# A strided sum over eight places in place of three sums over halves, in a sliding attention beside a feed-forward block

## The chip, the cores and the metric

The kernel runs on one core of a Trainium2 chip. The metric is the time of one execution on the device in microseconds (us), as the median of several runs. Engines are named as in the profile: PE is TensorE (matmuls; PEld are its weight loads, which overlap them), DVE is VectorE, ACT is ScalarE, POOL is GpSimd and SP is SyncE, which issues DMAs.

## What is computed

A block with two parallel branches on normalised rows, both in fp32 (2048 rows of 576, 32 heads of 18, a hidden width of 4608):

```python
xn = layernorm(x)
out = x + A(xn) + B(xn)

# A: each row attends to itself and the 7 rows 2, 4, ... 14 before it
idx = pos[:, None] - 2 * arange(8)[None, :]
logits = einsum("bhsd,bhswd->bhsw", q, k[:, :, idx]) * 18 ** -0.5   # -1e9 where idx < 0
attn = softmax(logits, axis=-1)
o = einsum("bhsw,bhswd->bhsd", attn, v[:, :, idx])
A = o_in_rows @ wo

# B
h = relu(xn @ w1 + b1) ** 2
B = h @ w2 + b2
```

The change concerns the line with `o`: for each row and each of its 576 columns, eight products of a weight and a value are summed.

## The kernel before

**Matmuls.** The rows are four blocks `b` of 512. All matrix products run on PE in a 32-bit form in which an operand is split into a high part (a rounded copy, made by ACT) and a low part (the rest, made by a subtraction on DVE); a product is the sum of high by high, high by low and low by high. The split of each weight tile therefore puts one ACT and one DVE instruction ahead of PE. The feed-forward part takes two blocks at a time and builds their first product from seven sub-products of halves instead of eight (`ffn_pair`, with `product` at L629 and `left` at L635); the second product is in `add` (L536). A pair of row blocks and a pair of hidden tiles make one call of `ffn_pair`, 18 calls for each half of the rows. The matmuls of L536 for one row block run beside these calls, seven at a time (`work(0)` to `work(3)`), and those of the other row block follow in loops of their own (`phase_b0` and `phase_b1`), 14 matmuls to a hidden tile.

**Handovers from DVE to PE** that the prediction speaks of:
- In `ffn_pair`, three PSUM banks `ba`, `bb` and `bc` hold the sub-products. DVE reads `bc` twice, at L725 (`r1`, the third sub-product added) and at L752 (`r0`). PE writes `bc` again at the B22 product (L745), right behind the first of these reads, and at the T1 product (L664) of the next call, behind the second. In the profile the reads are `r<-p,r`.
- `w1_lo` (L480) writes the low part of a `w1` tile, `w1s<-w1r,w1s`.
- `w2_lo` (L517) writes the low part of a `w2` or `wo` tile, `w2s<-w2r,w2s`. There are three such buffers. A hidden tile's 14 matmuls read first four high parts and then the low ones, so the fifth is the first that needs DVE's half.

**Attention** runs on DVE between these. The four groups of eight heads (`g`, 144 columns each) of a row block come from DRAM as tiles with four rows j of q to a partition and, for k and v, those and the fourteen rows before them (`fetch`, on POOL's queue). `attention(b, g)` is a generator. For each of four values of j it multiplies q with eight shifted rows of k into `pr` (128 partitions, 8 x 144 elements; `pr<-q,kv`) and reduces over the 18 columns of a head (L387). The softmax follows (L390 to L399). Then, again for each j, it multiplies the weights with eight shifted rows of v into `pr` (`pr<-lg,kv`, L405) and sums the eight places (L408 to L410), which leaves 144 columns in `q`. There is one buffer `pr`. After the fourth j POOL stores the result to DRAM (L415), from where a later step fetches it regrouped.

**Order of the work.** The order on each engine is written out by hand. The generator yields after each product and each sum, and the calls of `side(k)` in the loops (two, three or five between the handovers of a call of `ffn_pair`, one or two for each hidden tile of the loops) take that many units of whichever head group is in turn. The three sums over halves are one unit, as is the multiplication before them. DVE works off its instructions in this order, so a unit that takes longer delays all that stands behind it on DVE.

The helper `tt` (L108) records all two-operand instructions of DVE, so these carry its line and are told apart by their tiles.

Of the kernel before, what the change touches and what calls it, by code (L numbers as in the profile page):

```python
# [12 lines left out]
ALU = mybir.AluOpType  # L13
ET = mybir.EngineType
AX = mybir.AxisListType
# [30 lines left out]
def block_kernel(ctx: ExitStack, tc: tile.TileContext, x, xt, wqkv, wo, w1, b1, w2, b2, w1l, out):  # L46
    nc = tc.nc
# [12 lines left out]
    def kv_tile(n):  # L60
# [25 lines left out]
                            axis=AX.XY, op=ALU.add)  # L86
# [20 lines left out]
    def tt(out, a, b, op):  # L107
        return nc.vector.tensor_tensor(out=out, in0=a, in1=b, op=op)  # L108
# [232 lines left out]
    def shifted(t, j, *dims):  # L341
        a = t[:, j:j + 1, 0:1]
        return bass.AP(tensor=a.tensor, offset=a.offset, ap=[a.ap[0], [DIL * CG, W], *dims])
# [19 lines left out]
    def release():  # L363
        free[0] += 1
        fetch()

    def offer(b, g=None):
        if g is None:
            loads.append(("x", b, None))
            queue.append((("x", b), lambda: statistics(b)))  # L370
        else:
            loads.extend([("k", b, g), ("v", b, g)])
            queue.append((("k", b, g), lambda: attention(b, g)))
        fetch()

    def attention(b, g):
        k, q = landed.pop(("k", b, g)), landed.pop(("q", b, g))
        lg = sb.tile([P, NA, W], F32, name="lg")
        mx = sb.tile([P, NA], F32, name="mx")
        sm = sb.tile([P, NA], F32, name="sm")  # L380
        for j in range(NJ):
            pr = sb.tile([P, W, CG], F32, name="pr")
            tt(pr, q[:, j:j + 1].to_broadcast([P, W, CG]), shifted(k, j, [1, CG]), ALU.mult)
            if j == NJ - 1:
                release()
            yield
            nc.vector.tensor_reduce(out=lg[:, j * HG:(j + 1) * HG].rearrange("p a w -> p w a"),  # L387
                                    in_=pr.rearrange("p w (a d) -> p w a d", d=DH), axis=AX.X, op=ALU.add)
            yield
        if b == 0:  # L390
            l4 = lg[:4].rearrange("p (j h) w -> p j h w", j=NJ)
            tt(l4, l4, mask[:4, :, None].to_broadcast([4, NJ, HG, W]), ALU.add)
        nc.vector.tensor_reduce(out=mx, in_=lg, axis=AX.X, op=ALU.max)
        tt(lg, lg, mx[:, :, None].to_broadcast([P, NA, W]), ALU.subtract)
        yield "exp"
        nc.scalar.activation(lg, lg, AF.Exp, scale=SCALE)
        nc.vector.tensor_reduce(out=sm, in_=lg, axis=AX.X, op=ALU.add)
        nc.vector.reciprocal(sm, sm)
        tt(lg, lg, sm[:, :, None].to_broadcast([P, NA, W]), ALU.mult)  # L399
        yield  # L400
        v = landed.pop(("v", b, g))
        for j in range(NJ):
            pr = sb.tile([P, W, CG], F32, name="pr")
            at = lg[:, j * HG:(j + 1) * HG].rearrange("p a w -> p w a")
            tt(pr.rearrange("p w (a d) -> p w a d", d=DH), at[:, :, :, None].to_broadcast([P, W, HG, DH]),  # L405
               shifted(v, j, [DH, HG], [1, DH]), ALU.mult)
            yield
            tt(pr[:, :4], pr[:, :4], pr[:, 4:], ALU.add)  # L408
            tt(pr[:, :2], pr[:, :2], pr[:, 2:4], ALU.add)
            tt(q[:, j], pr[:, 0], pr[:, 1], ALU.add)  # L410
            if j == NJ - 1:
                for k, (a, z) in enumerate(OPART):
                    rows = oscr[b, k][g * L:(g + 1) * L].rearrange("l (j i) c -> l i j c", i=G)
                    for i in range(G):
                        nc.gpsimd.dma_start(rows[:, i], q[i * L:(i + 1) * L, :, a:z])  # L415
                release()
            yield
# [1203 lines left out]
```

## Time and profile before

| | |
|---|---|
| median of 3 runs | 1107.31 us (1107.31 to 1108.32) |
| profiled execution, its own time | 1107.93 us |
| its span, first to last instruction | 1106.2 us |
| PE busy | 1096.8 us, 99% |
| DVE busy | 912.0 us, 82% |
| ACT busy | 575.0 us, 52% |
| POOL busy | 115.4 us, 10% |
| granted TensorE clock | 1.000 |

A row of a group names line, engine and operation, then `out<-in` by the program's tile names, partitions x elements and type of output and input, and the count; behind the bars stand the busy time in us, the mean of one in ns, and the idle time of the engine just before them with what ended most of it. In a timeline a row begins with the start and the duration in us, rows of equal form are merged (x2 is two instructions), and idle time of over 0.1 us or so ahead of the row is given in brackets with what ended it. A row of the waits reads: who waited, for whom, us in total, times, the longest. A row of a window gives its length, then for PE, PEld, DVE, ACT and POOL the busy us and the number of instructions, then the granted clock, the DMA engines' share and GB/s. In the chain of waits a piece has its start, its length and the number of instructions.

### The profile page before, as it was taken

To read this page: it belongs to the slowest core of one execution; us is meant where nothing else is said; L and a number is where in the kernel's file an instruction comes from. 1 tells how busy PE (TensorE), PEld (TensorE's weight loads), DVE (VectorE), ACT (ScalarE), POOL (GpSimd) and SP (SyncE) were. 2 spreads that over 40 slices of the span, in tenths; PEclk is the share of its full clock that TensorE was granted. 3 is DMA by queue.
4 is the path that set the end of the run, shared out by engine and by line. 5 is a ranking of instruction groups with operands and counts; after the bars stand their busy time and mean duration, and the time that the engine had idled before them with its cause. 6 is when DMAs were issued, how large, how long until landed. Compare 5 with 4: busy or idle time off the path is not lost.

```text
span 1106.2 us, 13892 instructions
## 1 busy us (share of the span) xinstructions
PE 1096.8 (99%) x4950; PEld 925.2 (84%) x4950; DVE 912.0 (82%) x1223; ACT 575.0 (52%) x809; POOL 115.4 (10%) x219
## 2 busy tenths in 40 slices
PE   9999999999999999999999999999999999999998
PEld 7998888888888888888899887888888888888887
DVE  7696979897996979999979488978988789899654
ACT  5435666556566654455344355555555555533342
POOL 4000101020020100100010200202102021000100
PEclk9999999999999999999999999999999999999999
DMA  8956987889699686866755887768686785866752
GB/s 297 329 177 234 333 309 255 296 214 372 229 244 392 220 357 214 311 247 226 259 164 169 309 263 300 259 260 308 238 315 240 267 314 205 316 208 205 280 193 81
DMA packets 100279, 287.83 MB, mean 260 GB/s; under 512 B 13288, under 2 KB 41712, under 8 KB 85488
## 3 DMA queue, kind: packets, MB, share of 16 engines
q1 hardware_dynamic: 65280, 188.15, 49.1%
q0 software_dynamic: 10544, 52.14, 12.9%
q10 hardware_dynamic: 24384, 46.64, 12.6%
q8 instruction: 39, 0.64, 0.2%
q14 instruction: 32, 0.26, 0.1%
HBM read 205.14 MB, written 81.74 MB: 259 GB/s over the span
## 4 chain that ended last, share of the span: by engine, by line
PE 89%; DVE 5%; DMA 3%; ACT 1%; issue 1%; ACTq 0%; POOL 0%; DVEq 0%; POOLq 0%; SPq 0%
PE p L536 46%; PE p L629 31%; PE p L1041 5%; PE p L635 3%; DMA kvq<-st 2%; PE p L338 1%; PE p L1401 1%; PE p L1045 1%; DVE pr L108 1%; DMA kv<-kvq 1%; DVE lg L387 1%; DVE w1r L108 1%; DVE r L108 0%; PE p L1318 0%; DVE h L108 0%
## 5 line engine op out<-in xcount | busy, mean ns | idle before, releaser
L536 PE MATMUL p<-h,w2s 128*128 128x512 f32 x2066 | 491.4, 389 | 0.1
L536 PEld LDWEIGHTS p<-h,w2s 128*128 128x128 f32 x2066 | 387.5, 188 | 81.5 <-ACT h L642 0.6
L629 PE MATMUL p<-X,w1s 128*128 128x512 f32 x864 | 219.7, 389 | 1.2 <-DVE r L108 0.9
L629 PEld LDWEIGHTS p<-X,w1s 128*128 128x128 f32 x864 | 162.0, 188 | 35.6 <-DVE r L108 1.3
L509 ACT ACTIVATE w2s<-w2r 128x640 fp32r<-128x640 f32 x164 | 120.2, 735 | 116.1 <-PE p L536 87.6
L629 PE MATMUL p<-S,w1s 128*128 128x512 f32 x648 | 164.8, 390 | 1.5 <-ACT r L691 1.5
L108 DVE TENSOR_TENSOR w2s<-w2r,w2s 128x576 fp32r<-128x576 f32 x164 | 123.4, 753 | 40.6 <-ACT w2s L509 39.8
L629 PEld LDWEIGHTS p<-S,w1s 128*128 128x128 f32 x648 | 121.4, 188 | 27.4 <-ACT r L691 2.3
L415 POOL DMA_DIRECT2D o<-q x128 | 69.2, 605 | 584.8 <-DVE q L108 582.8
L638 ACT ACTIVATE r<-r,b1t 128x512 f32<-128x512 f32 x72 | 52.0, 723 | 126.9 <-DVE r L108 125.2
L387 DVE TENSOR_REDUCE lg<-pr 128x64 f32<-128x1152 f32 x64 | 86.5, 1352 | 1.5
L108 DVE TENSOR_TENSOR pr<-lg,kv 128x1152 f32<-128x1152 f32 x64 | 86.7, 1354 | 1.3
L108 DVE TENSOR_TENSOR pr<-q,kv 128x1152 f32<-128x1152 f32 x64 | 86.6, 1353 | 0.8
L108 DVE TENSOR_TENSOR pr<-pr 128x576 f32<-128x576 f32 (+1 forms) x128 | 77.5, 605 | 3.2
L646 ACT ACTIVATE r<-r 128x1024 f32<-128x1024 f32 x72 | 76.1, 1057 | 1.2
L108 DVE TENSOR_TENSOR h<-r,h 128x1024 fp32r<-128x1024 f32 (+3 forms) x46 | 51.8, 1136 | 27.0 <-ACT r L646 18.8
L108 DVE TENSOR_TENSOR r<-p,r 128x512 f32<-128x512 f32 (+1 forms) x77 | 52.9, 688 | 20.3 <-PE p L629 9.8
L108 DVE TENSOR_TENSOR w1s<-w1r,w1s 128x1024 fp32r<-128x1024 f32 (+1 forms) x42 | 50.3, 1198 | 16.5 <-ACT w1s L477 16.4
L691 ACT ACTIVATE r<-p 128x512 f32<-128x512 f32 x36 | 21.5, 597 | 70.9 <-PE p L629 70.5
L638 ACT ACTIVATE r<-p,b1t 128x512 f32<-128x512 f32 x72 | 48.3, 672 | 0.0
L108 DVE TENSOR_TENSOR h<-h 128x1024 fp32r<-128x1024 f32 x36 | 43.9, 1220 | 4.8 <-ACT h L938 4.6
L536 PE MATMUL p<-w1s,w2s 128*128 128x512 f32 x195 | 44.7, 389 | 0.0
(193 smaller groups left out, 1174.2 us busy)
## 6 DMA issues: line engine op xcount, KB each, us to landing
w2r<-in_w SPq DMA_DIRECT2D x144, 320.0 KB, 3.4
kv<-kvq POOLq DMA_DIRECT2D x29, 1296.0 KB, 9.4
w<-w1s SPq DMA_DIRECT2D x36, 1024.0 KB, 8.4
w1s<-w ACTq DMA_DIRECT2D x34, 1024.0 KB, 7.3
h<-r SPq DMA_DIRECT2D x36, 512.0 KB, 6.3
h<-h SPq DMA_DIRECT2D x36, 512.0 KB, 4.2
w1r<-in_w SPq DMA_DIRECT2D x18, 640.0 KB, 7.7
kvq<-st ACTq DMA_DIRECT2D x48, 216.0 KB, 3.2
```

The lines of the kernel that those rows point to most:

```text
L108: return nc.vector.tensor_tensor(out=out, in0=a, in1=b, op=op)
L338: nc.tensor.matmul(p[:, :QW], l, r, start=k == 0, stop=k == len(mm) - 1)
L387: nc.vector.tensor_reduce(out=lg[:, j * HG:(j + 1) * HG].rearrange("p a w -> p w a"), in_=pr.rearrange("p w (a d) -> p w a d", d=DH), axis ...
L415: nc.gpsimd.dma_start(rows[:, i], q[i * L:(i + 1) * L, :, a:z])
L509: nc.scalar.activation(w2s[stream[i]][:, :DE], raw2[i], AF.Copy)
L536: nc.tensor.matmul(yp[b][c], v, a, start=c not in yb[b], stop=c in last and c not in [o[0] for o in ops[i + 1:]], skip_group_check=True)
L629: nc.tensor.matmul(to, l, r, start=start and i == 0, stop=i == len(mm) - 1, skip_group_check=True)
L635: nc.tensor.matmul(to, weight(LEFT, k, f), v, start=False, stop=k == 1, skip_group_check=True)
L638: nc.scalar.activation(to, a, AF.Relu, bias=b1t[:, f:f + 1])
L646: nc.scalar.activation(r, r, AF.Square)
L691: nc.scalar.activation(u[:, 0], bb, AF.Copy)
L1041: nc.tensor.matmul(to, l[:, js], r, start=start and n == 0, stop=n == len(mm) - 1, skip_group_check=True)
```

## The change

In the second half of `attention`, the three sums over halves become one reduce:

```diff
             yield
-            tt(pr[:, :4], pr[:, :4], pr[:, 4:], ALU.add)
-            tt(pr[:, :2], pr[:, :2], pr[:, 2:4], ALU.add)
-            tt(q[:, j], pr[:, 0], pr[:, 1], ALU.add)
+            nc.vector.tensor_reduce(out=q[:, j], in_=pr.rearrange("p w c -> p c w"), axis=AX.X, op=ALU.add)
             if j == NJ - 1:
```

Before, the first sum adds places 4 to 7 to places 0 to 3 (576 elements), the second places 2 and 3 to 0 and 1 (288), and the third the last two (144), the first two in place. After, one instruction reads the 1152 elements of `pr` once, for each column its eight places one after the other, and writes 144 sums. Each column's places lie 144 elements, that is 576 bytes, apart. `pr` is no longer overwritten. The order of the eight additions is another one. What runs on PE, ACT, POOL and SP, and in which order, is the same in both kernels; all lines behind L410 move up by two.

On DVE ahead of the first call of `ffn_pair`'s split weights (`w1s` is the split tile of `w1`, `w1r` its source, `pr` the products, `lg` the softmax weights, `kv` the tile of v), before:

```order
L108 TENSOR_TENSOR pr<-lg,kv 128x1152
L108 TENSOR_TENSOR w1r<-w1r 128x512
L108 TENSOR_TENSOR w1r<-w1r 128x256 x2
L108 TENSOR_TENSOR pr<-pr 128x576
L108 TENSOR_TENSOR pr<-pr 128x288
L108 TENSOR_TENSOR q<-pr 128x144
L108 TENSOR_TENSOR w1s<-w1r,w1s 128x1024 x2
```

and after:

```order
L408 TENSOR_REDUCE q<-pr 128x144
L108 TENSOR_TENSOR pr<-lg,kv 128x1152
L108 TENSOR_TENSOR w1r<-w1r 128x512
L108 TENSOR_TENSOR w1r<-w1r 128x256 x2
L408 TENSOR_REDUCE q<-pr 128x144
L108 TENSOR_TENSOR w1s<-w1r,w1s 128x1024 x2
```

The three adds ahead of `w1s` are one reduce in their place, as are the three of the unit before (the first row after).

On DVE within a later call of `ffn_pair`, ahead of a read of bank `bc` (`r_3260<-p_3186,r_3228`, and `r_3222<-p_3152,r_3190` after; the numbers of the buffers differ, since fewer instructions come before), before:

```order
L108 TENSOR_TENSOR pr<-lg,kv 128x1152
L108 TENSOR_TENSOR pr<-pr 128x576
L108 TENSOR_TENSOR pr<-pr 128x288
L108 TENSOR_TENSOR q<-pr 128x144
L108 TENSOR_TENSOR w2s<-w2r,w2s 128x576
L108 TENSOR_TENSOR w1s<-w1r,w1s 128x1024
L108 TENSOR_TENSOR w2s<-w2r,w2s 128x576
L108 TENSOR_TENSOR r_3260<-p_3186,r_3228 128x512
```

and after:

```order
L108 TENSOR_TENSOR pr<-lg,kv 128x1152
L408 TENSOR_REDUCE q<-pr 128x144
L108 TENSOR_TENSOR w2s<-w2r,w2s 128x576
L108 TENSOR_TENSOR w1s<-w1r,w1s 128x1024
L108 TENSOR_TENSOR w2s<-w2r,w2s 128x576
L108 TENSOR_TENSOR r_3222<-p_3152,r_3190 128x512
```

The read of the bank stands behind the same units as before; only the sum itself is another instruction. In the last quarter (`phase_b1`), where units of attention alternate with `w2_lo` and `h_lo` (`h<-h`), the same: three rows become one, and the rest keeps its place.

## The prediction

> **What bounds the kernel now.** I read the page's totals first, then the list of waits for PE alone, then the costs of the operations that the change touches, then timelines at the places where DVE hands something to PE.
>
> The first lines of the page, with busy time and its share of the span for each engine:
>
> ```profile
> span 1106.2 us, 13892 instructions
> PE 1096.8 (99%) x4950; PEld 925.2 (84%) x4950; DVE 912.0 (82%) x1223; ACT 575.0 (52%) x809; POOL 115.4 (10%) x219
> ```
>
> PE is the bound. DVE has 1106 - 912 = 194 us without work, so its own sum could grow a good deal before DVE became the bound as a whole. The change touches DVE alone, so it can shorten the kernel only by shortening what PE waits for. The waits of PE, longest first in total:
>
> ```profile
> PE p L1318 <- DVE lg L1311: 2.1, 1, 2.1
> PE p L629 <- ACT r L691: 1.5, 2, 0.8
> PE p L629 <- DVE r L108: 0.9, 1, 0.9
> PE p L629 <- DVE w1s L108: 0.3, 1, 0.3
> ```
>
> The first stands ahead of all attention. Only the last, 0.3 us, has the changed sums right ahead of it (below). So there is next to nothing to gain on PE, and much to lose: a slower DVE meets a PE that never rests. **The question is what one reduce costs against three adds, and how much of a difference PE's handovers let through.**
>
> **The price of one edit.** 64 times (4 row blocks, 4 head groups, 4 values of j), three adds become one reduce. The rows that bear on it, from the groups with shapes kept apart (count, busy us, mean ns):
>
> ```profile
> L387 DVE TENSOR_REDUCE lg<-pr 128x64 f32<-128x1152 f32 x64 | 86.5, 1352 | 1.5
> L108 DVE TENSOR_TENSOR pr<-pr 128x576 f32<-128x576 f32 x64 | 48.2, 753 | 1.0
> L108 DVE TENSOR_TENSOR pr<-pr 128x288 f32<-128x288 f32 x64 | 29.3, 458 | 2.2
> L108 DVE TENSOR_TENSOR q<-pr 128x144 f32<-128x144 f32 x64 | 19.7, 308 | 2.5 <-DVE pr L108 0.3
> L393 DVE TENSOR_REDUCE mx<-lg 128x32 f32<-128x256 f32 x16 | 6.7, 417 | 0.3
> L1335 POOL TENSOR_TENSOR h<-w1r,h 128x432 fp32r<-128x432 f32 x2 | 2.2, 1118 | 0.0
> ```
>
> Removed: 753 + 458 + 308 = 1519 ns of busy time; with the small gaps between dependent instructions the three hold DVE about 1.6 us (in the rows below the next instruction starts 1.62 us and 1.51 us after the first add). Added: one reduce over 1152 elements. The two reduces of before give its form: (1352 - 417) / (1152 - 256) = 1.04 ns for an element, and 417 - 256 x 1.04 = 150 ns fixed. But both read neighbours: their innermost dimension goes on by 4 bytes. The new one reads `p c w`: its innermost step is from one of the eight places to the next, 144 elements or 576 bytes away, for every element. No row of before reads so.
>
> So the price is bounded. From below: 1.35 us, the same instruction on as many elements with neighbours. No reduce here does better than one element a step of 1.04 ns, so I exclude less. From above: POOL's subtraction streams the slowest, 1118 / 432 = 2.59 ns an element, which would be 2.98 us for 1152. If an element costs whole steps, only two prices lie in between: one step, 1.35 us, and two, 150 + 2 x 1152 x 1.04 = 2.55 us. **I take two steps, 2.55 us**: by its reading pattern the new instruction resembles none of the one-step rows, and 2.55 is the whole-step price nearest to the upper end. This is a choice and not a reading, so one step stays a rival with a large chance. With two steps a sum costs 2.55 - 1.6 = 0.95 us more, 64 x 0.95 = 61 us of DVE in all; with one step 1.35 - 1.6 = -0.25 us, 16 us less.
>
> [...]
>
> **What of 61 us reaches PE.** The instruction order on PE, ACT, POOL and SP is the same before and after; on DVE each three rows become one in place, nothing is moved past a queue, and no wait is added, on PE or elsewhere. POOL's stores of q at L415 wait for the last sum of a head group and start by its lag later; the list of PE's waits above has none on POOL or on a load of attention, so I cost that at nothing; without that cover a head group's first product would come later by the lag. So the loss is DVE's lag behind PE at each handover, less the idle time ahead of it, less the slack with which DVE delivers now.
>
> *First FFN pair.* DVE, then PE (start, duration):
>
> ```profile
> 86.00 1.24 DVE L108 TENSOR_TENSOR pr<-pr 128x576 f32<-128x576 f32 x2
> ...
> 90.41 1.24 DVE L108 TENSOR_TENSOR pr<-pr 128x576 f32<-128x576 f32 x2
> ...
> 91.92 2.40 DVE L108 TENSOR_TENSOR w1s<-w1r,w1s 128x1024 fp32r<-128x1024 f32 x2
> ```
>
> ```profile
> 93.19 1.21 PE L629 MATMUL p<-X,w1s 128*128 128x512 f32 x4 [0.29 <-DVE w1s L108]
> ```
>
> PE waits already, with two sums ahead on DVE and no idle between. Both count in full: 2 x 0.95 = **1.9 us**.
>
> *FFN pairs with three sums ahead of a handover.* A pair's second sum in PSUM bank `bc` is read by DVE (r<-p, L725), and PE may write the bank again only then, at the B22 product (L745). One such pair:
>
> ```profile
> 355.85 1.24 DVE L108 TENSOR_TENSOR pr<-pr 128x576 f32<-128x576 f32 x2
> ...
> 361.58 1.25 DVE L108 TENSOR_TENSOR pr<-pr 128x576 f32<-128x576 f32 x2
> 362.86 0.31 DVE L108 TENSOR_TENSOR q<-pr 128x144 f32<-128x144 f32 x1
> 363.20 1.36 DVE L108 TENSOR_TENSOR pr<-lg,kv 128x1152 f32<-128x1152 f32 x1
> 364.60 1.25 DVE L108 TENSOR_TENSOR pr<-pr 128x576 f32<-128x576 f32 x2
> 365.88 0.31 DVE L108 TENSOR_TENSOR q<-pr 128x144 f32<-128x144 f32 x1
> 366.11 0.75 DVE L108 TENSOR_TENSOR w2s<-w2r,w2s 128x576 fp32r<-128x576 f32 x1
> ...
> 368.58 0.68 DVE L108 TENSOR_TENSOR r<-p,r 128x512 f32<-128x512 f32 x1
> ```
>
> ```profile
> 370.48 1.52 PE L629 MATMUL p<-X,w1s 128*128 128x512 f32 x6
> ```
>
> The read ends at 369.26, PE's next product in the bank starts at 370.48: a slack of 1.2 us. Three sums bring 2.85 us. About 0.4 us of idle time lies between them, so some 2.4 us of lag arrive and about 1.2 us stall PE. There are five such pairs (the reads at 227.13, 297.85, 368.58, 700.58 and 839.81): 5 x 1.2 = **6 us**. Pairs with two sums ahead, or with lag carried over, lose less, for instance
>
> ```profile
> 738.00 1.25 DVE L108 TENSOR_TENSOR pr<-pr 128x576 f32<-128x576 f32 x2
> ...
> 752.55 0.69 DVE L108 TENSOR_TENSOR r<-p,r 128x512 f32<-128x512 f32 x1 [0.30 <-ACT r L723]
> ```
>
> ```profile
> 754.89 1.30 PE L629 MATMUL p<-X,w1s 128*128 128x512 f32 x5
> ```
>
> Three sums (738.00, 741.49, 746.68) less 0.3 us of idle time less 754.89 - 753.24 = 1.65 us of slack: 0.9 us. I count four like it (with the reads at 120.76, 191.26 and 892.17), 1 us each: **4 us**. The other pairs have one sum or none ahead and as much slack, and give nothing.
>
> *The last quarter.* The densest stretch of DVE, then the chain's long piece on PE, then DVE at the first sum and from the last one on:
>
> ```profile
> 978.00:1032.00 54.00, 54.00 (x240) 44.71 (x239) 53.07 (x70) 21.45 (x27) 4.35 (x8) 1.00 0.58 188
> ```
>
> ```profile
> 950.21 150.36 PE p L536 x663
> ```
>
> ```profile
> 978.22 1.24 DVE L108 TENSOR_TENSOR pr<-pr 128x576 f32<-128x576 f32 x2
> ...
> 1030.48 1.24 DVE L108 TENSOR_TENSOR pr<-pr 128x576 f32<-128x576 f32 x2
> 1031.76 0.31 DVE L108 TENSOR_TENSOR q<-pr 128x144 f32<-128x144 f32 x1
> 1031.98 1.42 DVE L108 TENSOR_TENSOR w2s<-w2r,w2s 128x576 fp32r<-128x576 f32 x2
> ```
>
> DVE is busy 53.07 of 54 us (third figure after the length) and PE all 54. Eight sums lie in it: 8 x 0.95 = 7.6 us with nothing to absorb them but slack. PE's 663 matmuls take 150.36 / 663 = 0.227 us each. The first 100 end the third row block (7 + 28 + 65), so tile n of the last one starts at 972.9 + 14 n x 0.227; tile 19 at 1033.2, and its fifth matmul, the first to read the lower half that DVE writes, at 1034.1. DVE finishes that half, the first of the two at 1031.98, at 1032.7. So 1.3 us are left, and 7.6 - 1.3 = **6.3 us** go to PE.
>
> *Between these stages* stand twelve sums (408 to 612 us). Most lie where DVE rests; I count **1 us** there, with 0 and 3 as ends.
>
> Sum: 1.9 + 6 + 4 + 6.3 + 1 = 19.2 us. The profiled execution took 1107.93 us (span 1106.2 and 1.7 around it), 0.6 above the median of 1107.31. 1107.9 + 19.2 = **1127 us**. With all pair terms gone 1107.9 + 9 = 1117; with slack used up by other lags, 2.85 for a three-sum pair and 1.9 for a two-sum one, 1.9 + 14 + 7.6 + 6.3 + 1, that is 31 us, or 1138.
>
> **The rivals.** *One step an element* (ends on the other side: not slower). The reduce then costs what L387 costs, 1352 ns on as many elements. DVE gets 16 us shorter, PE only the 0.29 us at 93.19: 1107.6. It decides from one point: below 1.6 us for the reduce the kernel isn't slower at all. For it speaks that every streaming DVE row above fits 1.04 ns an element; against it, that every one reads neighbours. [...]
>
> *Two steps, but hidden.* DVE's 194 idle us swallow the lag at most handovers, and only the places without idle time pay part: 1109 to 1117, about 1112. Against it: the two places without any idle time, 93.19 and 978 to 1032, give 8 us by themselves.
>
> *More than two steps.* At 2.98 us or above a sum costs 1.4 us more or worse, and since the slack is spent once, most of the extra 0.45 us x 40 sums in dense places goes through: 1127 + 18 = 1145.
>
> That the change does nothing is excluded: the DVE order shows 64 reduces in place of 192 adds.
>
> **How the numbers follow.** Two steps as worked out 0.55 (1117 to 1138); one step 0.31 (1106 to 1109, nearly all within 0.2%, or 2.2 us, which is about what a measurement of this kernel can tell from no change); two steps hidden 0.07; more than two 0.07. The cases of no change and of slower hold most of it, so the range spans both: 1106 to 1138, which leaves out the dearest case. The likeliest one's own range is 1117 to 1138. Faster by over 0.2%: 0.04, part of the one-step case. Within 0.2%: 0.26. Slower by over 0.2%: 0.70.
>
> **What would show it.** The group of the new reduce q<-pr decides first: a mean near 2550 ns is my case, near 1350 ns the rival. Then DVE's busy time (912 + 64 x (2.55 - 1.52) = 978, or 901), new waits of PE on DVE r near the pairs named and on w2s between 978 and 1032, and 1.9 us more at the first pair. If the mean is right and PE's waits sum to far less than 19 us, the slack was misread; if waits stand elsewhere, in ACT's chain behind `r` say, I left out a handover.

## The result, and the profile after

The changed kernel takes **1122.07 us** (median of 4 runs, 1121.79 to 1124.52) against 1107.49 us (1107.31 to 1108.32) for the kernel before on the same chip: a ratio of 1.0134, interval 1.0119 to 1.0149. It is slower by some 14.6 us. The profiled execution took 1121.79 us, with a span of 1120.1.

The page's first lines for the changed kernel, as shown for the one before:

```profile
span 1120.1 us, 13760 instructions
PE 1102.6 (98%) x4950; PEld 925.1 (83%) x4950; DVE 949.6 (85%) x1095; ACT 576.1 (51%) x809; POOL 116.2 (10%) x219
```

DVE grew from 912.0 to 949.6 us, that is 0.59 us for each of the 64 sums. PE's own busy time grew too, from 1096.8 to 1102.6, with the same 4950 matmuls; a part of that is explained below. The group of the new instruction:

```profile
L408 DVE TENSOR_REDUCE q<-pr 128x144 f32<-128x1152 f32 x64 | 139.4, 2178 | 1.0
```

Its mean of 2178 ns is neither one step an element (1352) nor two (2550). And the longest waits of PE, in the form in which they were shown for the kernel before:

```profile
PE p L633 <- DMA w1s<-w: 3.6, 1, 3.6
PE p L534 <- DVE w2s L108: 2.8, 5, 0.9
PE p L627 <- DVE r L108: 2.5, 5, 0.9
PE p L1316 <- DVE lg L1309: 2.1, 1, 2.1
PE p L627 <- ACT r L689: 0.7, 1, 0.7
```

The second and third rows are the lag of DVE that the prediction spoke of (0.9 us of the third was there before). The first is new and no step of the prediction has it: PE waits once, 3.6 us, for a **DMA**.

Since PE works off the same matmuls in the same order in both kernels, the start of each matmul can be compared with its own start before. The difference grows only where time is lost; the last column is its growth since the place above:

| place (time before, us) | difference there, us | grown by |
|---|---|---|
| first FFN pair, 93.19 | +0.1 | 0.09 |
| handover of bank `bc`, 229.04 | +0.5 | 0.43 |
| 273.92, between two of them | +0.9 | 0.42 |
| handovers of bank `bc`, 299.76 and 370.48 | +1.6, +2.1 | 0.61 + 0.56 |
| `add` between the stages, 413 to 544 | +4.2 | 2.06 |
| 630.21, where PE used to wait 0.85 us for ACT | +3.3 | -0.88 |
| **631.70 to 633.64** | **+8.5** | **5.18** |
| handover of bank `bc`, 702.53 | +9.5 | 0.99 |
| last quarter, 996 to 1049 | +13.7 | 4.27 |

**The new wait.** PE's timeline of the changed kernel there:

```profile
633.50 1.52 PE L627 MATMUL p<-S,w1s 128*128 128x512 f32 x6
638.58 1.19 PE L633 MATMUL p<-x,w1s 128*128 128x512 f32 x2 [3.56 <-DMA w1s<-w]
639.57 2.69 PE L627 MATMUL p<-X,w1s 128*128 128x512 f32 x6
...
642.56 1.54 PE L627 MATMUL p<-X,w1s 128*128 128x512 f32 x6
```

Six matmuls of one form take 1.52 us ahead of the wait, 2.69 right behind it, and 1.54 three us later: behind the pause PE runs for a while at about half its rate, which costs another 1.6 us (the difference grows from +6.9 at the wait's end to +8.5). That is where some of PE's additional busy time comes from. The granted clock says the same: 1.00 from 632 to 636 us, and then (third figure from the end)

```profile
636.00:640.00 4.00, 1.42 (x3) 1.14 (x4) 1.88 (x2) 0.00 (x0) 0.00 (x0) 0.83 1.03 398
```

A mean of 0.83 over these four microseconds fits half the clock for 1.4 of them, and PE starts again 1.4 us before their end.

What PE waits for is the second half of a `w1` tile, which `w1_again` (L485, L487 before) loads back on SP's queue in the middle of the program. POOL loads there too: a tile of k (`kv<-kvq`, L360) and the regrouped result of attention (`kv<-o`, L843, L845 before). POOL's timeline before, then SP's issue of the reload with its size and its time to landing:

```profile
616.93 0.77 POOL L360 DMA_DIRECT2D kv<-kvq  x1
617.48 0.76 POOL L845 DMA_DIRECT2D kv<-o  x1
```

```profile
620.49 0.46 SPq L487 DMA_DIRECT2D w1s<-w  x1
```

```profile
w1s<-w SPq DMA_DIRECT2D x1, 1024.0 KB, 11.1
```

It landed at 620.49 + 11.1 = 631.6, and PE used it at once, before:

```profile
631.70 0.70 PE L635 MATMUL p<-x,w1s 128*128 128x512 f32 x2
```

The same two timelines after, and the reload as a piece of the chain (start, length):

```profile
619.40 4.33 POOL L413 DMA_DIRECT2D o<-q  x8 [30.00 <-DVE q L408]
623.52 0.76 POOL L360 DMA_DIRECT2D kv<-kvq  x1
624.16 0.66 POOL L843 DMA_DIRECT2D kv<-o  x1
```

```profile
624.79 0.43 SPq L485 DMA_DIRECT2D w1s<-w  x1
```

```profile
624.79 13.75 DMA w1s<-w
```

POOL's loads stand on its queue behind the eight stores of a head group's result (L413), and these wait for DVE's last sum of that group: the bracket names it. Before, the first load is issued 3.56 us ahead of the reload; after, 1.27 us ahead, since four longer sums lie in the group. POOL's two loads land at 623.9 and 626.4 before, the later of them 5.9 us into the reload, and at 630.3 and 632.7 after, 7.9 us into it. The DMA engines' share is 0.98 to 1.04 from 628 to 640 us (0.99 to 1.05 before, from 620 to 632). The reload takes 13.7 us in place of 11.1, that is 2.6 more. It is also issued 4.3 us later than before, while PE is 3.3 us later there. Since it had no slack, 2.6 + 4.3 - 3.3 = 3.6 us are PE's wait.

### The profile page after: what moved, and what is told of

Its sections match the earlier page's. It is cut to its first block, busy times and chain, and to the rows that moved or that the text cites. A ratio compares the mean times of both kernels' runs of the same rounds, so it can differ in the third digit from the quotient of the medians.

```text
span 1120.1 us, 13760 instructions
## 1 busy us (share of the span) xinstructions
PE 1102.6 (98%) x4950; PEld 925.1 (83%) x4950; DVE 949.6 (85%) x1095; ACT 576.1 (51%) x809; POOL 116.2 (10%) x219
## 4 chain that ended last, share of the span: by engine, by line
PE 68%; DVE 18%; DMA 5%; issue 5%; ACT 3%; DVEq 0%; ACTq 0%; SPq 0%; POOL 0%; POOLq 0%
PE p L534 31%; PE p L627 25%; PE p L1039 6%; DVE pr L108 3%; DVE q L408 3%; DVE h L108 2%; DVE w2s L108 2%; PE p L633 2%; DMA w<-w1s 2%; PE p L338 1%; DVE w1s L108 1%; DVE r L108 1%; DMA w1s<-w 1%; DVE w1r L108 1%; DMA h<-h 1%
## 5 line engine op out<-in xcount | busy, mean ns | idle before, releaser
L408 DVE TENSOR_REDUCE q<-pr 128x144 f32<-128x1152 f32 x64 | 139.4, 2178 | 1.0
L413 POOL DMA_DIRECT2D o<-q x128 | 69.2, 605 | 609.2 <-DVE q L408 607.2
L387 DVE TENSOR_REDUCE lg<-pr 128x64 f32<-128x1152 f32 x64 | 86.5, 1352 | 1.5
```

The lines of the kernel that those rows point to most:

```text
L408: nc.vector.tensor_reduce(out=q[:, j], in_=pr.rearrange("p w c -> p c w"), axis=AX.X, op=ALU.add)
```

## The experiments

My theory A: the sums' own lag accounts for some 10 of the 14.6 us, and the rest is this **collision**, which one head group triggers (the one of row block 1, group 0), whose last sum releases POOL's stores and loads at 612 to 624. The rivals are in the expectations.

**Strided reduce in that head group alone** (four of the 64 sums):

```diff
-            tt(pr[:, :4], pr[:, :4], pr[:, 4:], ALU.add)
...
+            if (b, g) == (1, 0):
+                nc.vector.tensor_reduce(out=q[:, j], in_=pr.rearrange("p w c -> p c w"), axis=AX.X, op=ALU.add)
+            else:
+                tt(pr[:, :4], pr[:, :4], pr[:, 4:], ALU.add)
...
```

> The kernel before, with the strided reduce in the one head group (row block 1, group 0) whose four sums stand right before the regroup loads of the middle stage; all other head groups keep the three adds. Theory A (collision): four sums 0.57 us longer each make POOL's stores and the loads behind them 2.3 us later against PE, these meet the w1 reload on SP's queue, and PE waits 3 us or more for it and then runs some matmuls at half rate: 1110.5 to 1113 us. Rival B (the wait in the middle stage comes from something earlier, or from chance in the DMA queues): within 0.5 us of the kernel before, 1107 to 1108, with no wait of PE on a DMA.

Measured: 1113.97 us against 1108.49 us, ratio 1.0045 (1.0028 to 1.0062). The longest of PE's waits, and the reload as a piece of the chain:

```profile
PE p L638 <- DMA w1s<-w: 4.3, 1, 4.3
```

```profile
622.12 14.47 DMA w1s<-w
```

Four sums that are 0.6 us longer each cost 5.5 us, 1 us above theory A's range and far above B's. A holds: the loss is not spread over the sums. Not all of it is the collision. In the profiled execution (1115.19 us) PE falls back by 2.3 us between 489 and 548 us, which is the four sums' own lag; it gets 1.1 us back at 630, where it used to wait for ACT, and loses 6.8 us at the reload, by the wait and the slow matmuls behind it.

**Strided reduce in all the others** (the same edit with `!=`):

> The changed kernel, with the three adds back in that one head group (row block 1, group 0). Theory A: PE's wait for the w1 reload of 3.6 us and the slow matmuls after it go: 1117 to 1118.5 us. Rival B: as the changed kernel, 1121.5 to 1122.5 us, with the wait still there.

Measured: 1118.04 us against 1108.49, ratio 1.0086 (1.0071 to 1.0101). PE's waits that changed:

```profile
PE p L632 <- DVE r L108: 2.6, 5, 0.9
...
PE p L632 <- ACT r L694: 2.1, 3, 0.8
PE p L539 <- DVE w2s L108: 1.9, 4, 0.6
PE p L632 <- DVE w1s L108: 0.7, 1, 0.7
```

No wait of PE for a DMA is left, and the time lies in theory A's range. The two parts add up, 5.5 + 9.5 = 15.0 us beside 14.6 for the whole change.

**The three adds, and an idle fourth of 432 neighbours** makes the sum as long as the reduce without a strided read:

```diff
             tt(pr[:, :4], pr[:, :4], pr[:, 4:], ALU.add)
+            tt(pr[:, 4:7], pr[:, 4:7], pr[:, 4:7], ALU.add)
             tt(pr[:, :2], pr[:, :2], pr[:, 2:4], ALU.add)
```

> The kernel before, with one more add of neighbours (3 x 144 elements, result not used further) between the first and the second of the three adds of every sum, so that a sum holds DVE about 0.6 us longer, as the strided reduce does, without any strided read. Theory A (only the length of the sum counts): 1120 to 1124 us, with PE's waits at the same places as in the changed kernel. Rival C (the strided read also slows other engines or DMAs at SBUF): under 1115 us.

Measured: 1122.53 us against 1108.49, ratio 1.0126 (1.0111 to 1.0142). The added instruction, and PE's longest wait:

```profile
L108 DVE TENSOR_TENSOR pr<-pr 128x432 f32<-128x432 f32 x64 | 38.9, 608 | 2.2
```

```profile
PE p L636 <- DMA w1s<-w: 4.9, 1, 4.9
```

C falls: the time is that of the changed kernel without any strided read. PE loses time at nearly all the places of the changed kernel, and 1.2 us each at the first FFN pair and at 330.36 (time of before), where the changed kernel loses next to nothing; some handovers lose less. Single places differ by up to 2 us, so a small harm of the strided read beside its length isn't excluded.

**What a strided read costs**, by itself: behind the end of the kernel before, a list of reduces over 8 x 144 elements with the eight places at different distances (lines 1592 to 1610), with other counts of places at 576 bytes (1616, 1617), and products and copies; for instance

```diff
+    [f(out=a, in_=b, axis=X, op=add) for a, b in red(1, 3)]
```

> The kernel before, and behind its end a list of single DVE instructions on unused tiles: reduces of 144 columns over 8 places with the places 1 to 288 elements apart, reduces over 4, 2 and 16 places 144 apart, and products, adds and copies of 1152 elements that read or write far apart. [...] Rival M (banks: the distance of 144 is an unlucky multiple): distances such as 143, 145, 146 or 148 cost nearer 1350 ns than 2180 ns. The products that write 32 bytes apart are open; if writes are free they take 1355 ns.

Measured (the whole took 1360.88 us, which says nothing of the sums). Distances of 4, 8, 12, 16, 576 and 608 bytes, then two and sixteen places, 576 bytes apart:

```profile
L1592 DVE TENSOR_REDUCE q<-kv 128x144 f32<-128x1152 f32 x4 | 5.1, 1346 | 0.0
L1593 DVE TENSOR_REDUCE q<-kv 128x144 f32<-128x1152 f32 x4 | 5.1, 1348 | 0.0
L1594 DVE TENSOR_REDUCE q<-kv 128x144 f32<-128x1152 f32 x4 | 6.7, 1746 | 0.0
L1595 DVE TENSOR_REDUCE q<-kv 128x144 f32<-128x1152 f32 x4 | 8.3, 2148 | 0.0
L1606 DVE TENSOR_REDUCE q<-kv 128x144 f32<-128x1152 f32 x4 | 8.1, 2076 | 0.0
L1610 DVE TENSOR_REDUCE q<-kv 128x144 f32<-128x1152 f32 x4 | 11.4, 2914 | 0.0
L1616 DVE TENSOR_REDUCE q<-kv 128x144 f32<-128x288 f32 x4 | 1.5, 444 | 0.0
L1617 DVE TENSOR_REDUCE q<-kv 128x144 f32<-128x2304 f32 x4 | 15.7, 3994 | 0.0
```

M falls: at distances of 143, 145, 146 and 148 elements the reduce took 2074 to 2078 ns. The dearer price starts with the distance, between 8 and 16 bytes, and is then nearly the same (2074 to 2207 ns) at every distance tried up to 1152 bytes but one (608 bytes, 2914 ns, which stays unexplained). From 1152 to 2304 elements it is (3994 - 2076) / 1152 = 1.66 ns an element, 1.6 of the prediction's steps of 1.04 ns. Two places cost nothing more: 150 + 288 x 1.04 = 450 ns. Another layout of `pr` doesn't help either. The list has products of 1152 elements in six forms, three of each, one form with neighbours alone:

```profile
L1586 DVE TENSOR_TENSOR pr<-kv 128x1152 f32<-128x1152 f32 x18 | 36.2, 2012 | 0.6
```

The shortest took 1345 ns, the longest 2229. With 1345 for the three with neighbours and 2229 at most for twelve others, the three that write their results 576 bytes apart took at least (36.2 - 4.0 - 26.8) / 3 = 1.8 us each. With a sum over neighbours (1.35) that is 3.15 us, more than the product (1.35) and the three adds (1.52) of before.

**The one-step rival, run.** A reduce over eight neighbouring places:

```diff
-            tt(pr[:, :4], pr[:, :4], pr[:, 4:], ALU.add)
-            tt(pr[:, :2], pr[:, :2], pr[:, 2:4], ALU.add)
-            tt(q[:, j], pr[:, 0], pr[:, 1], ALU.add)
+            nc.vector.tensor_reduce(out=q[:, j], in_=pr.rearrange("p w c -> p (w c)").rearrange("p (c w) -> p c w", w=W), axis=AX.X, op=ALU.add)
```

> The changed kernel, but its reduce adds eight neighbours of the products (places 4 bytes apart) in place of the eight places of a column: as many elements, the same 144 results, in the wrong grouping. So this computes another sum, and only its time counts. Theory A (only the length of the sum counts, and the length hangs on the distance): the reduce takes 1350 ns, the 16 us that DVE gains are worth nothing to PE, 1106.5 to 1108.5 us. Rival D (the change costs time by its form, one instruction in place of three, whatever it reads): 1118 us or more.

Measured: 1113.04 us against 1107.84, ratio 1.0047 (1.0033 to 1.0061). Both expectations missed: the sum is shorter than the three adds, DVE has 10 us less to do (901.7), and the kernel is 5.2 us slower. The group, and PE's longest wait:

```profile
L408 DVE TENSOR_REDUCE q<-pr 128x144 f32<-128x1152 f32 x64 | 86.2, 1348 | 1.0
```

```profile
PE p L627 <- ACT st L1048: 4.8, 1, 4.8
```

The chain shows who made ACT late, a store of projected rows (`kvq<-st`, L1052) that frees ACT's stage buffer, and POOL's timeline shows why:

```profile
616.67 10.71 DMA kvq<-st
...
627.49 0.54 ACT st L1048
```

```profile
615.74 0.76 POOL L360 DMA_DIRECT2D kv<-kvq  x1
616.48 0.57 POOL L843 DMA_DIRECT2D kv<-o  x1
```

The same store before, as a DMA issue with its time to landing:

```profile
kvq<-st SPq DMA_DIRECT2D x1, 216.0 KB, 2.4
```

Before, POOL's loads (616.93) are issued 0.04 us behind this store (616.89), which lands in 2.4 us. With the shorter sum they come 1.2 us earlier, so the store stands behind 0.93 us of them and takes 10.7 us. So in this place the kernel loses when POOL comes later and when it comes earlier.

**That reading, tested:** the near reduce everywhere but in that head group (the edit as above, with `if (b, g) != (1, 0)` ahead of it and the three adds in the other case).

> The sum is one reduction over eight neighbouring places (another sum than the reference's: wrong places are added), 1348 ns each, in all head groups but one: row block 1, group 0 keeps the three adds, so that POOL's loads in the middle of the program start when they do before. Theory A: the 5 us that the near reduce lost everywhere come from the one store of the projected rows that POOL's loads overtook there, and a shorter sum is otherwise worth nothing, since TensorE seldom waits for VectorE: 1106.5 to 1108.5 us, VectorE about 902 us busy, the 4.8 us wait of TensorE for the copy of the projected rows gone. Rival D: the form with one instruction costs by itself, wherever it stands: 1111 us or more, with waits of TensorE spread over several places.

Measured: 1107.95 us against 1107.91, ratio 0.9998 (0.9988 to 1.0008). A holds and D falls: with POOL's timing kept, the wait for ACT is gone, and sixty sums that are shorter than three adds are worth nothing. PE's longest waits are those of the kernel before:

```profile
PE p L1321 <- DVE lg L1314: 2.1, 1, 2.1
PE p L632 <- ACT r L694: 1.4, 2, 0.7
PE p L632 <- DVE r L108: 0.9, 1, 0.9
```

**Half of the change**: the first add stays, and one strided reduce over four places takes the place of the other two.

```diff
             tt(pr[:, :4], pr[:, :4], pr[:, 4:], ALU.add)
-            tt(pr[:, :2], pr[:, :2], pr[:, 2:4], ALU.add)
-            tt(q[:, j], pr[:, 0], pr[:, 1], ALU.add)
+            nc.vector.tensor_reduce(out=q[:, j], in_=pr[:, :4].rearrange("p w c -> p c w"), axis=AX.X, op=ALU.add)
```

> The kernel before, with the first of the three adds kept and the other two replaced by one strided reduce over the four places left (576 elements, 576 bytes apart). The micro list gives 1115 ns for it, so a sum holds DVE 753 + 1115 ns, about 0.3 us longer than before and 0.3 us shorter than in the changed kernel. Theory A: the slack of 1.2 us and more takes most of it, and the time lies well below the middle of the two kernels, 1108 to 1113 us. Rival E (the loss is in proportion to the length of the sums): 1114 to 1116 us.

Measured: 1119.9 us against 1107.84, ratio 1.0108 (1.0094 to 1.0122), above both expectations. DVE is busy 935.3 us, less than after, and it is PE's waits for others that make it dear:

```profile
PE p L628 <- ACT r L690: 3.5, 2, 2.8
PE p L634 <- DMA w1s<-w: 3.4, 1, 3.4
```

By its trace, ACT waits 6.20 us ahead of the first for a store (`h<-r`) that is issued at 315.79 and takes 17.2 us to land. Two loads of POOL's are issued 0.53 us ahead of it and 0.06 us behind it, but that is so in the kernel before too, where the store takes 15.5 us and nobody waits. What the longer sums change is when it is issued, 2.9 us later than before: on SP's queue it stands behind `mr<-mr`, which waits for POOL's L144, and that for DVE's statistics (`mv`, L139), which stand behind sums on DVE. The rest, 1.7 us more to land, stays open: in the changed kernel the same store is issued 3.3 us later than before, takes 13.7 us, and PE doesn't wait. The start of the matmul behind this wait, 330.36 in the kernel before, tells the same: PE loses 0.9 us there with all groups but one changed, 1.2 us in the padded kernel and nothing in the changed one, so the wait comes and goes. No run took it apart.

**The reload earlier.** The second half is issued four steps of the loop earlier, on SP's queue right behind the first half, and so ahead of POOL's loads:

```diff
-                if (s, i) == (4, 1):
+                if (s, i) == (3, 1):
                     w1_again(NP, 1, nc.sync)
```

In the kernel before:

> The kernel before, with the second reload of w1 in the middle stage issued four steps of the quad loop earlier (one line moved: at step (3, 1) in place of (4, 1)), ahead of two of the stores on SP's queue. Theory A (the reload is late because POOL's loads fill the DMA engines first): the wait of 0.85 us at 630 can shrink, 1106 to 1108 us, from 0.1% faster to no change. Rival: the move delays the stores and the kernel gets slower by 0.5 us or more.

Measured: 1107.97 us against 1107.84, ratio 1.0004 (0.9995 to 1.0013), no difference, although the wait of 0.85 us at 630 is gone from its trace. In the changed kernel:

> The changed kernel with the same reload moved. Theory A: it lands before PE needs it, PE's wait of 3.6 us and the matmuls at half rate behind it go, 1116.5 to 1119 us. Rival B (PE would wait there for something else just as long): 1121 to 1123 us.

Measured: 1118.42 us against 1107.84, ratio 1.0096 (1.0082 to 1.0109). The wait for the DMA is gone and what is left is DVE's lag:

```profile
PE p L534 <- DVE w2s L108: 3.1, 5, 1.2
PE p L627 <- DVE r L108: 2.5, 5, 0.9
```

Theory A holds, and the collision alone is thus worth some 4 us of the 14.6 (10.6 are left). No version was found that beats the kernel before.

## Why the prediction was right in direction, and where its steps failed

The forecast was slower, 1127 us with a range of 1106 to 1138; measured were 1122.07. The mechanism (a longer sum on DVE, which a PE without rest meets at the handovers) is shown by the runs for some 10 of the 14.6 us; sizes were off in both directions, and one step failed.

- **"I take two steps, 2.55 us": mis-sized.** The reduce takes 2.18 us, so a sum costs 0.57 to 0.59 us more, not 0.95. The step of whole steps an element was wrong: it is 1.6 of them. No row of before reads at such a distance, so the two steps were an estimate of mine. The list of strided reads has the price at each distance: 1348 ns at 8 bytes, 1746 at 12, 2148 at 16 and 2076 at 576. With two places it doesn't rise (444 ns).
- **First FFN pair, 1.9 us: 1.2 on DVE, 0.1 on PE.** In the profile before, the matmul starts at 93.19, after at 93.28, which looks as if the term were nothing. DVE from the first of the two sums to the split weights, after (the rows before, at 86.00 and 91.92, stand in the prediction):

```profile
84.90 2.17 DVE L408 TENSOR_REDUCE q<-pr 128x144 f32<-128x1152 f32 x1
92.01 2.35 DVE L108 TENSOR_TENSOR w1s<-w1r,w1s 128x1024 fp32r<-128x1024 f32 x2
```

  From the first sum to `w1s` it is 5.92 us before and 7.11 after: both sums count in full, 2 x 0.6, and only the price was too high. But the first sum starts 1.1 us earlier after, before anything changed has run, so the loss is hidden. Two other profiles of the changed order start it at 84.67 and 84.74, three others with the three adds at 85.06, 85.21 and 86.00: the start varies by as much as the term.
- **Five pairs with three sums, 6 us: 2.6.** Four of the five pay, 0.4 to 1.0 us each; the one at 839.81 doesn't. With 0.57 the working of the prediction gives 3 x 0.57 - 0.4 - 1.2 = 0.1 each. What it left out is the restart of PE, about 0.3 us at each stall (below); why the one at 702.53 pays twice as much as the others is open.
- **Four pairs with two sums, 4 us: 0**, as that working gives with the right price: even the three sums of its example bring only 3 x 0.57 - 0.3 = 1.4 us, less than the slack of 1.65. One handover that I had not counted, at 273.92, paid 0.42.
- **Between the stages, 1 us with 0 and 3 as ends: 2.1**, inside.
- **Last quarter, 6.3 us: 4.3.** Eight sums bring 8 x 0.57 = 4.6, less 1.3 of slack is 3.3, and four or five restarts bring the rest. The place and the releaser (`w2s`) were right:

```profile
1005.97 29.31 PE L534 MATMUL p<-h,w2s 128*128 128x512 f32 x126 [0.32 <-DVE w2s L108]
1035.94 6.66 PE L534 MATMUL p<-h,w2s 128*128 128x512 f32 x28 [0.66 <-DVE w2s L108]
1043.16 3.48 PE L534 MATMUL p<-h,w2s 128*128 128x512 f32 x14 [0.56 <-DVE w2s L108]
1047.04 15.26 PE L534 MATMUL p<-h,w2s 128*128 128x512 f32 x66 [0.40 <-DVE w2s L108]
```

- **"So I cost that at nothing" (POOL's stores behind the last sum): the step that failed.** I saw that POOL's stores move with the sum, and looked only for who waits for POOL. POOL's own loads stand behind those stores, and they share the DMA engines (busy share 0.98 to 1.04 there) with a load that PE does wait for. That is 5.2 us in the table and 4.3 net of the wait for ACT that it covers; it is 4.0 by the run that moved the reload out of the way, and 5.5 where the four sums were changed alone, their own lag included.

With 0.57 in place of 0.95 the prediction's own working comes to 1.1 + 0.5 + 0 + 3.3 + 1 = 6 us; some ten restarts of 0.3 us bring it to 9, and the two runs without the collision measured 9.5 and 10.6. The collision is 4 to 5 more. That the forecast of 19.2 came near 14.6 is partly luck: a price too high made up for two costs left out.

**The rivals.** One step an element falls by the price. Its 1107.6 us was wrong as well: built, it took 1113.04, because the same POOL loads moved the other way. "Below 1.6 us for the reduce the kernel isn't slower at all" was thus no bound. "Two steps, but hidden" (1112) falls: the lag alone costs 9.5 to 10.6 us. More than two steps falls by the price.

## What to carry to other kernels

Replacing instructions by fewer can pay only if the one reads its elements as cheaply: here one sum over eight places 12 bytes or more apart (1746 ns and up) costs DVE more than three sums over halves that each read neighbours (1519). And it pays only where somebody waits for it: sixty sums of 1.35 us in place of 1.6 were worth nothing to a PE that was busy 99% of the time. When an instruction that is off the bound gets longer or shorter, follow what its end releases (stores, and the loads behind them in the queue) and ask which transfers they then share the DMA engines with; in this kernel a shift of one or two microseconds in either direction cost 5. A change that touches all rounds of a loop is best tried in one round and in all the others: if the parts don't scale with their counts (here 5.5 us for 4 sums and 9.5 for 60), the loss sits in one place.

## What the runs showed of the hardware

- **PE's restart.** The loss at a stall is larger than its wait row. The handover at 370.48 before is this one after:

```profile
372.59 1.66 PE L627 MATMUL p<-X,w1s 128*128 128x512 f32 x6 [0.24 <-DVE r L108]
```

The matmul ahead of this wait of 0.24 us starts 1.70 us later than before, the second behind it 2.22 us: 0.52 us are lost. At 1047.04 above, a wait of 0.40 us goes with 12.48 and 13.15, so 0.67. About 0.3 us come on top: the matmul ahead ends alone, without the next one overlapping it (a single one has 0.39 us in the rows, while in a series they start 0.227 apart), and the first two behind start some 0.34 us apart.
- **PE's clock.** Behind a wait of 3.56 us the matmuls started 0.427 us apart for some eight matmuls, in place of 0.227, at a granted clock of 0.50 from 640 to 642 us; behind 2.77 us (the kernel with half of the change) likewise, after four matmuls at the full rate. Behind 0.81 us (711.99 in the changed kernel) six matmuls took 1.66 us, at a granted clock of 1.00. With waits of up to 1.2 us on DVE's `w2s`, in the changed kernel with the reload moved, the mean granted clock is 1.000.
- **DMA order.** A store of 216 KB landed in 2.4 us when two loads were issued 0.04 and 0.6 us behind it, and in 10.7 us when they were issued 0.9 and 0.2 us ahead of it.
